# One drain for K instead of a masked double one, with the odd heads' rows copied by DMA

## The chip, the cores and the metric

The kernel runs on one core of a Trainium2 chip. The core has a matrix engine (TensorE, PE in the profile), which writes to PSUM, and three engines that compute on rows: VectorE (DVE), ScalarE (ACT) and GpSimd (POOL). SyncE (SP) issues the DMAs here. Each engine runs its own list of instructions in order and waits on semaphores for the others. The metric is the time of one execution on the device in microseconds; lower is better.

## What is computed

Two layers, applied twice in turn with the same weights, on x of 2048 tokens by 512, in bf16:

```python
def _A_ref(x, wqkv, wo):                       # attention; H = 32, Dh = 16, W = 256
    qkv = transpose((x @ wqkv).reshape(B, S, 3, H, Dh), 2, 0, 3, 1, 4)
    q, k, v = qkv[0], qkv[1], qkv[2]
    scores = jnp.einsum("bhqd,bhkd->bhqk", q, k) * (Dh ** -0.5)
    mask = (i - j >= 0) & (i - j < W)
    p = _softmax(jnp.where(mask, scores, -1e9))
    return (p @ v, heads joined) @ wo

def _B_ref(x, w1, b1, w2, b2):                 # MLP; F = 1792
    return _gelu(x @ w1 + b1) @ w2 + b2

x = x + _A_ref(_layernorm(x), A_wqkv, A_wo)
x = x + _B_ref(_layernorm(x), B_w1, B_b1, B_w2, B_b2)
x = x + _A_ref(_layernorm(x), A_wqkv, A_wo)
x = x + _B_ref(_layernorm(x), B_w1, B_b1, B_w2, B_b2)
```

Each query sees the 256 keys up to its own. There are 32 heads of only 16 dimensions.

## The kernel before

**Tiles.** x stays on chip (`X`). The two passes make 32 token tiles of 128 (tau = 0..31; 16 to 31 are the second pass), two tiles make an attention block (b = 0..15, blocks 8 to 15 the second pass). Per block: `lnq` normalises both tiles, transposes them into `xnTA` and projects Q into `QT`; `kv` projects K into `KT` and V into `Va`; `attention` does the scores, the exponential, the mask and the product with V; `outproj` adds the result to `X` and normalises for the MLP. The MLP runs in ten jobs (`JOBS`, J = 0..9) of two or four tiles (`mlp`).

**K and the heads.** `QT` and `KT` hold the head dimensions on the 128 partitions, four chunks c of 128, so a chunk has eight heads of 16 rows. The array is cut into pieces of 32 rows by 64 columns for the scores, and 32 rows hold two heads: rows 32r to 32r+15 the even one, 32r+16 to 32r+31 the odd one. For a score to see one head alone, the other head's rows of K must be zero. So `kv` writes K twice (line 1031): one VectorE instruction reads the PSUM bank [128, 512] twice, multiplies by `parmask` and writes `KT[:, kb, 0]` with the odd heads' rows zero and `KT[:, kb, 1]` with the even heads' rows zero. There are two such instructions per block (i = 0, 1, for chunks 2i and 2i+1), 32 in all. `KT` has two buffers (KB = 2): block b uses kb = b % 2.

**Scores.** A block's scores are one stream of positions, head pair by head pair, even (par 0) and then odd (par 1), cut into visits of 512 columns (`visit`; ten per block, six in blocks 7 and 15). A visit is 16 or 24 matmuls (8 per piece: two halves h, four row groups r) into four PSUM banks; two ScalarE exponentials of [128, 1024] take them to `E` (line 1112). Masks on `E` run on VectorE or GpSimd (line 1133). The product with V (`pv`) takes two phases per chunk pair and is transposed by VectorE (line 1198), normalised (1203, VectorE or GpSimd) and transposed again (1208).

**Layernorm.** `layernorm` computes mean and variance on VectorE (lines 934 and 936), variance + epsilon on VectorE (938), the power -0.5 on GpSimd (941), and the scaled row on VectorE (944). Layernorms ahead of the MLP of tiles 4 to 29 then go through DRAM: a transpose on VectorE into `xs_` (953), four DMAs into `scr_x` (957) and one from there into `xnTB` (961). All of those are on SP's queue.

**What sets the order.** The kernel builds 3295 operations with `add` (engine, function, an assumed duration, what is read and written, and possible other engines, `alt`). A written list, `ORDER` (line 635), gives the order in which they are put on their engines; x stands for operation x, and -1-x for operation x on its other engine. `_Plan.follow` goes through the list and picks PSUM banks; `_Sched` adds the semaphore waits that the reads and writes need. SP's DMAs use twelve semaphores in turn, and a DMA waits for the one twelve before it. `evac` (line 915) is the helper that drains a PSUM bank on VectorE (line 917) or, for the kinds in `ACT_OK`, on ScalarE (line 919).

Line 32 (`_Slots.matmul`) issues all matmuls, so the profile tells them apart by their tiles: `ps<-QT,KT` are scores, `ps<-E,Va` the product with V, `ps<-xnTA,Wqkv_sb` Q and K projections, `ps<-Wqkv_sb,xnTA` V, `ps<-Wo_sb,OT` the output projection, `ps<-xnTB,W_sb` and `ps<-W_sb,gT` the MLP.

Of the kernel before, what the change touches and what calls it, by code (L numbers as in the profile page):

```python
# [7 lines left out]
ALU = mybir.AluOpType  # L8
# [510 lines left out]
def bass_interleave_layers__sliding_block__dense_activation_gelu__prompt_kernel(  # L519
# [16 lines left out]
    Dh = 16  # L536
    H = D // Dh
    HC = P // Dh
    RG = HC // 2
# [7 lines left out]
    EPS = 1e-5  # L547
# [11 lines left out]
    KB = 2  # L559
# [20 lines left out]
    ACT_OK = "oqv"  # L580
# [12 lines left out]
    with ExitStack() as kctx:  # L593
        S_ = _Sched(nc, kctx)

        def sb(name, shape, dtype=dt.bfloat16):
# [275 lines left out]
        def dma(fn, writes, reads=(), dur=2200.0, prio=0.0, issue=640.0):  # L872
            add("sp", fn, dur, reads=reads, writes=writes, prio=prio, dma=True, geo=issue)
# [486 lines left out]
```

## Time and profile before

| | us |
|---|---|
| time, median of 3 runs | 459.97 (459.38 to 460.35) |
| the profiled execution's own time | 460.33 |
| its span, first to last instruction | 458.5 |
| PE busy | 442.5 |
| ACT busy | 394.7 |
| DVE busy | 362.1 |
| POOL busy | 257.6 |
| exponentials, 304 | 286.4, mean 1046 ns |
| K drains (line 1031), 32 | 38.6, mean 1211 ns |
| score matmuls, 2976 | 64.8 |
| DMA into scr_x, 104 of 32 KB, issue to landing | 1.6 |
| DMA into xnTB, 26 of 128 KB, issue to landing | 2.1 |

Busy times are those of the profiled execution; instructions that overlap are counted once, so 304 exponentials of 1046 ns fill 286.4 us. Matmuls overlap too: their distance from start to start is what they cost TensorE. A line of a group reads: line, engine, operation, output<-inputs, shape, count, then busy us and mean ns of one, then the engine's idle time just before them and what ended it. PEld is the load of a matmul's stationary side, which runs beside other matmuls.

### The profile page before, as it was taken

The page shows a single profiled execution, that of the slowest core. Times are in us where ns is not written, and L with a number is a line of the kernel's source. Part 1 is how long each engine was busy: PE and PEld are TensorE (multiplying, and loading weights), DVE is VectorE, ACT ScalarE, POOL GpSimd, SP SyncE. Part 2 cuts the span into 40 slices and gives each one's busy share as a digit, 9 for nine tenths or more (in the row PEclk, how much of TensorE's full clock was granted, in tenths as well). Part 3 has the DMA queues.
Part 4 walks back from the last instruction along what each step waited for, and adds up shares of the span by engine and source line. Part 5 has one row for each costly group of instructions (what it writes and reads, how often), then busy time and mean ns, then how long its engine had stood idle before and what let it go on. Part 6 is the DMA issues. An engine that isn't in the chain of part 4 may idle for free.

```text
span 458.5 us, 19397 instructions
## 1 busy us (share of the span) xinstructions
PE 442.5 (97%) x8793; PEld 235.6 (51%) x8793; DVE 362.1 (79%) x712; ACT 394.7 (86%) x475; POOL 257.6 (56%) x290
## 2 busy tenths in 40 slices
PE   7998899999889999999999999999999999999997
PEld 4554554655444455555445545556454554444663
DVE  5999888788997789886989788787787967777412
ACT  2999999999989989899997999979997999784442
POOL 4476665863656766664589464783556625563200
PEclk9999999999999999999999999999999999999999
DMA  7570000011010021100110102001020012002101
GB/s 229 195 279 4 4 3 3 5 18 33 16 34 3 9 44 23 29 11 17 26 49 3 24 14 48 16 9 44 11 51 3 11 40 40 23 5 70 59 23 59
DMA packets 27856, 18.18 MB, mean 40 GB/s; under 512 B 15868, under 2 KB 27260, under 8 KB 27772
## 3 DMA queue, kind: packets, MB, share of 16 engines
q1 hardware_dynamic: 27772, 16.92, 13.8%
q8 instruction: 69, 1.13, 1.0%
q14 instruction: 15, 0.12, 0.1%
HBM read 11.41 MB, written 5.51 MB: 37 GB/s over the span
## 4 chain that ended last, share of the span: by engine, by line
PE 71%; ACT 11%; DVE 9%; DMA 6%; SPq 2%; issue 1%; DVEq 0%
PE ps L32 70%; ACT E L1112 10%; DMA scr_x<-xs_ 2%; DMA xnTB<-scr_x 2%; DMA X<-in_A_x_dram 2%; DVE E L1133 1%; DVE stat L934 1%; PE ps L36 1%; SPq L957 1%; DVE KT L1031 1%; DVE Va L917 1%; DVE xn L944 1%; DVE xs_ L953 1%; ACT gT L1279 1%; DVE X L991 1%
## 5 line engine op out<-in xcount | busy, mean ns | idle before, releaser
L1112 ACT ACTIVATE E<-ps 128x1024 bf16<-128x1024 f32 x304 | 286.4, 1046 | 25.5 <-PE ps L32 24.6
L1133 POOL TENSOR_TENSOR E<-E,mask 128x512 bf16<-128x512 bf16 (+1 forms) x159 | 165.5, 1058 | 96.7 <-ACT E L1112 42.8
L32 PE MATMUL ps<-W_sb,gT 128*128 128x512 bf16 x448 | 117.6, 380 | 0.1
L32 PE MATMUL ps<-xnTB,W_sb 128*128 128x512 bf16 (+1 forms) x560 | 116.1, 337 | 1.2 <-DMA xnTB<-scr_x 0.8
L32 PEld LDWEIGHTS ps<-xnTB,W_sb 128*128 128x128 bf16 x560 | 50.7, 98 | 47.4 <-ACT E L1112 3.6
L991 DVE TENSOR_TENSOR X<-X,ps 128x512 bf16<-128x512 bf16 x64 | 43.4, 681 | 37.8 <-PE ps L32 37.2
L32 PE MATMUL ps<-QT,KT 32*64 32x320 bf16 (+4 forms) x2976 | 64.8, 258 | 6.0 <-ACT E L1112 5.3
L32 PE MATMUL ps<-xnTA,Wqkv_sb 128*128 128x256 bf16 x512 | 69.3, 274 | 1.0 <-DMA Wqkv_sb<-in_A_wqkv_dram 0.5
L1279 ACT ACTIVATE gT<-ps,b1T 128x512 bf16<-128x512 f32 (+1 forms) x92 | 48.7, 590 | 16.9 <-PE ps L32 16.4
L32 PEld LDWEIGHTS ps<-W_sb,gT 128*128 128x128 bf16 x448 | 39.5, 98 | 43.6 <-issue 5.9
L941 POOL TENSOR_TENSOR rstd<-veps,mhalf 128x1 f32<-128x1 f32 x64 | 36.8, 579 | 33.5 <-DVE veps L938 33.1
L32 PEld LDWEIGHTS ps<-xnTA,Wqkv_sb 128*128 128x128 bf16 x512 | 45.8, 98 | 18.9 <-issue 4.5
L32 PEld LDWEIGHTS ps<-QT,KT 32*64 32x64 bf16 x2976 | 27.2, 103 | 52.5 <-ACT E L1112 36.8
L1198 DVE STREAM_TRANSPOSE TT<-ps 128x1024 f32<-128x1024 f32 x32 | 39.9, 1246 | 14.2 <-PE ps L32 13.7
L32 PE MATMUL ps<-E,Va 64*17 64x128 bf16 (+3 forms) x3872 | 49.0, 230 | 1.8 <-POOL E L1133 0.5
L32 PEld LDWEIGHTS ps<-E,Va 64*17 64x17 bf16 x3872 | 39.3, 85 | 18.9 <-PE ps L32 6.8
L1242 POOL TENSOR_TENSOR X<-X,b2b 128x512 bf16<-128x512 bf16 x32 | 37.4, 1173 | 17.5 <-DVE xn L944 7.5
L1133 DVE TENSOR_TENSOR E<-E,mask 128x512 bf16<-128x512 bf16 (+1 forms) x103 | 41.7, 432 | 6.7 <-ACT E L1112 6.3
L934 DVE BATCH_NORM_STATS2 stat<-X 128x6 f32<-128x512 bf16 x64 | 43.7, 686 | 3.8 <-DMA X<-in_A_x_dram 2.8
L1031 DVE TENSOR_TENSOR KT<-ps,parmask 128x1024 bf16<-128x1024 f32 x32 | 38.6, 1211 | 4.7 <-PE ps L32 4.5
L1267 DVE TENSOR_SCALAR gT<-ps,b1T 128x512 bf16<-128x512 f32 (+1 forms) x48 | 31.9, 673 | 6.6 <-PE ps L32 6.0
L32 PE MATMUL ps<-Wqkv_sb,xnTA 128*128 128x512 bf16 x128 | 35.3, 381 | 0.2 <-DVE Va L917 0.2
(49 smaller groups left out, 331.3 us busy)
## 6 DMA issues: line engine op xcount, KB each, us to landing
W_sb<-in_B_w_dram SPq DMA_DIRECT2D x2, 1792.0 KB, 12.8
scr_x<-xs_ SPq DMA_DIRECT2D x104, 32.0 KB, 1.6
xnTB<-scr_x SPq DMA_DIRECT2D x26, 128.0 KB, 2.1
out_dram<-X SPq DMA_DIRECT2D x16, 128.0 KB, 1.8
Wqkv_sb<-in_A_wqkv_dram SPq DMA_DIRECT2D x3, 512.0 KB, 6.7
X<-in_A_x_dram SPq DMA_DIRECT2D x3, 512.0 KB, 4.9
X<-in_A_x_dram SPq DMA_DIRECT2D x2, 256.0 KB, 2.9
Wo_sb<-in_A_wo_dram SPq DMA_DIRECT2D x1, 512.0 KB, 6.5
```

Source lines behind the costliest of these rows:

```text
L32: return self.e.matmul(*a, **k)
L36: return self.e.transpose(*a, **k)
L934: add("dve", lambda e, B: e.bn_stats(stat6[:, k6, :], X[:, t, :]), 590, reads=["X%d" % t], writes=["st%d" % k6], prio=prio)
L941: add("pool", lambda e, B: e.tensor_tensor(out=rstd[:, k : k + 1], in0=veps[:, k : k + 1], in1=mhalf[:], op=ALU.pow), 535, reads=["ve%d" % ...
L991: add("dve", lambda e, B: e.tensor_tensor(out=X[:, t, :], in0=X[:, t, :], in1=ps[:, B[g][0], :], op=ALU.add), d_psum(512), reads=["X%d" % ...
L1031: add("dve", lambda e, B, g=g, i=i: e.tensor_tensor(out=KT[:, kb, :, 2 * i : 2 * i + 2, :].rearrange("p a c q -> p a (c q)"), in0=ps[:, B[ ...
L1112: add("act", lambda e, B, g_=g_, gi=gi: e.activation(E[:, 2 * gi : 2 * gi + 2, e0 : e0 + 512], ps[:, B[g_][0] : B[g_][0] + 2, :], AF.Exp, ...
L1133: op = lambda e, B, Ew=Ew, Mw=Mw: e.tensor_tensor(out=Ew, in0=Ew, in1=Mw, op=ALU.mult)
L1198: add("dve", lambda e, B: e.transpose(TT[:, s].rearrange("p a c q d -> p (a c q d)"), ps[:, B[g][0] : B[g][0] + 2, :].rearrange("p a n -> ...
L1242: add("pool", lambda e, B: e.tensor_tensor(out=X[:, t, :], in0=X[:, t, :], in1=b2b[:], op=ALU.add), 1110, reads=["X%d" % t, "b2b"], writes ...
L1267: add("dve", lambda e, B, g=g, fc=fc: e.tensor_scalar(out=gT[:, fc, 0:M], in0=ps[:, B[g][0], 0:M], scalar1=b1T[:, fc : fc + 1], scalar2=No ...
L1279: add("act", lambda e, B, g=g, fc=fc: e.activation(gT[:, fc, 0:M], ps[:, B[g][0], 0:M], AF.Gelu_apprx_tanh, bias=b1T[:, fc : fc + 1], scal ...
```

## The change

From block 2 on (`KDMA`), K's PSUM bank is drained once, unmasked, into `KT[:, kb, 0]`, by `evac` on VectorE or ScalarE ("k" joins `ACT_OK`). The even heads' scores read rows 32r to 32r+15 of it only, 16 rows instead of 32. For the odd heads, four DMAs (one per row group r) copy rows 32r+16 to 32r+31 from `KT[:, kb, 0]` to `KT[:, kb, 1]`, where the other rows are still zero from blocks 0 and 1, which keep the masked form. Blocks 2 and 3 (`KBOTH`) copy after each half i, 16 rows x 2 chunks; later blocks copy all four chunks after the second half. That makes 64 DMAs more. A score of an odd head waits for the copies of its chunk, all four of them.

In `layernorm`, variance + epsilon may also run on GpSimd. The list `ORDER` is new, of 3359 entries. In it, 8 of the 28 single K drains are on ScalarE and 34 of the 64 variance + epsilon on GpSimd; of masks, 7 double and 3 single ones pass from GpSimd to VectorE, 5 normalisations (line 1203) from VectorE to GpSimd, and 2 V drains and 4 drains of transposed x from ScalarE to VectorE.

```diff
-    ACT_OK = "oqv"
+    ACT_OK = "oqvk"
+    KDMA = KB
+    KBOTH = 4
...
         ORDER = [
...
         ]
...
-            add("dve", lambda e, B: e.tensor_scalar(
-                out=veps[:, k : k + 1], in0=statmv[:, k, 1:2], scalar1=EPS, scalar2=None, op0=ALU.add), 75,
-                reads=["mv%d" % k], writes=["ve%d" % k], prio=prio - 300)
+            eps = lambda e, B: e.tensor_scalar(
+                out=veps[:, k : k + 1], in0=statmv[:, k, 1:2], scalar1=EPS, scalar2=None, op0=ALU.add)
+            add("dve", eps, 75, reads=["mv%d" % k], writes=["ve%d" % k], prio=prio - 300, alt=(("pool", eps, 130, 0.0),))
...
+                if b >= KDMA:
+                    evac(lambda B, i=i: KT[:, kb, 0, 2 * i : 2 * i + 2, :].rearrange("p c q -> p (c q)"),
+                         lambda B, g=g: ps[:, B[g][0], :], 512, ["ps:" + g], ["K%d_0_%d" % (kb, 2 * i + c) for c in range(2)],
+                         prio, free=[g], kind="k")
+                    lo = 2 * i if b < KBOTH else 0
+                    if i or b < KBOTH:
+                        for r in range(RG):
+                            dma(lambda e, B, lo=lo, hi=2 * i + 2, r=r: e.dma_start(
+                                KT[32 * r + Dh : 32 * r + 2 * Dh, kb, 1, lo:hi, :], KT[32 * r + Dh : 32 * r + 2 * Dh, kb, 0, lo:hi, :]),
+                                ["K%d_1_%d%s" % (kb, c, "abcd"[r]) for c in range(lo, 2 * i + 2)],
+                                reads=["K%d_0_%d" % (kb, c) for c in range(lo, 2 * i + 2)],
+                                prio=prio, dur=2200.0, issue=400.0)
+                    continue
...
-                        rd += ["K%d_%d_%d" % (kb, par, c)] + ["Q%d_%d" % (qi, c) for qi in qb]
+                        rd += (["K%d_1_%d%s" % (kb, c, x) for x in "abcd"] if par else ["K%d_0_%d" % (kb, c)]) + ["Q%d_%d" % (qi, c) for qi in qb]
...
-                                rows = slice(32 * r, 32 * r + 32)
+                                rows = slice(32 * r, 32 * r + (32 if par or b < KDMA else Dh))
```

More of the change, by code (lines that the diff above doesn't have):

```diff
@@ L1029, in kv @@
                 prio = kprio + pair[i]
-                proj(g, 1, i, xs, xr, prio, ["K%d_%d_%d" % (kb, par, 2 * i + c) for par in range(2) for c in range(2)], "m1" if b < 1 else "o")
+                proj(g, 1, i, xs, xr, prio, ["K%d_0_%d" % (kb, 2 * i + c) for c in range(2)] + ["K%d_1_%d%s" % (kb, 2 * i + c, x) for c in range(2) for x in "abcd"], "m1" if b < 1 else "o")
+                if b >= KDMA:
[11 more added lines that the diff above has]
+                    continue
                 add("dve", lambda e, B, g=g, i=i: e.tensor_tensor(
@@ L1035, in kv @@
                     reads=["ps:" + g, "parmask"],
-                    writes=["K%d_%d_%d" % (kb, par, 2 * i + c) for par in range(2) for c in range(2)],
+                    writes=["K%d_0_%d" % (kb, 2 * i + c) for c in range(2)] + ["K%d_1_%d%s" % (kb, 2 * i + c, x) for c in range(2) for x in "abcd"],
                     prio=prio, free=[g])
```

362 rows, old and new, of the table ORDER are left out of this document.

## The prediction

> **What bounds the kernel now.** I read the page first, then busy time by stage, then the waits, then the timeline at the places where the waits lie. Page, parts 1 and 4 (busy shares; the chain that ended last):
>
> ```profile
> span 458.5 us, 19397 instructions
> PE 442.5 (97%) x8793; PEld 235.6 (51%) x8793; DVE 362.1 (79%) x712; ACT 394.7 (86%) x475; POOL 257.6 (56%) x290
> ...
> PE 71%; ACT 11%; DVE 9%; DMA 6%; SPq 2%; issue 1%; DVEq 0%
> ```
>
> VectorE, the engine that the change unloads, carries 9% of the chain. Where the chain lies is seen in the busy time of three stretches (us, then busy us of PE, PEld, DVE, ACT, POOL):
>
> ```profile
> 0.00:13.50 13.50, 10.95 (x82) 6.27 (x83) 8.39 (x24) 4.62 (x7) 5.06 (x20) 1.00 0.63 199
> 13.50:131.00 117.50, 108.11 (x2537) 62.41 (x2542) 106.28 (x227) 114.91 (x140) 74.38 (x80) 1.00 0.19 57
> 131.00:459.00 328.00, 323.48 (x6184) 166.97 (x6184) 247.41 (x463) 275.13 (x330) 178.11 (x191) 1.00 0.11 27
> ```
>
> From the first exponential (13.5) to 131, ScalarE works 114.9 of 117.5 us: its queue sets the pace, and TensorE idles 9.4 us. From 131 on, TensorE works 323.5 of 328 us, and 2.9 us of the rest lie behind the last matmul (residual, output). The clock is 1.00 everywhere. What TensorE waited for from 131 on (total, times, longest):
>
> ```profile
> PE ps L32 <- DMA xnTB<-scr_x: 0.8, 2, 0.5
> PE ps L32 <- ACT E L1112: 0.6, 1, 0.6
> PE ps L32 <- DVE Va L917: 0.2, 1, 0.2
> ```
>
> So only 1.6 us can be won there by shorter waits; K's drain is not among them. ScalarE's own waits between 13.5 and 131:
>
> ```profile
> ACT E L1112 <- PE ps L32: 1.9, 4, 1.0
> ACT QT L919 <- PE ps L32: 0.5, 2, 0.3
> ```
>
> **The change part by part.** The order list names every operation by its number in build order, a negative entry choosing the other engine; counting both lists gives what moves.
>
> *K's drain.* Rows (mean ns after the bar's busy us):
>
> ```profile
> L1031 DVE TENSOR_TENSOR KT<-ps,parmask 128x1024 bf16<-128x1024 f32 x32 | 38.6, 1211 | 4.7 <-PE ps L32 4.5
> L917 DVE CAST Va<-ps 128x512 bf16<-128x512 f32 x22 | 14.8, 676 | 1.0 <-PE ps L32 0.8
> L919 ACT ACTIVATE Va<-ps 128x512 bf16<-128x512 f32 x10 | 6.1, 612 | 0.0
> L938 DVE TENSOR_SCALAR veps<-statmv 128x1 f32<-128x1 f32 x64 | 9.0, 146 | 1.1
> ```
>
> Blocks 0 and 1 keep the masked form (4 drains). The other 28 x 1.211 = 33.9 us become 20 x 0.676 = 13.5 on VectorE, by V's row (same shapes), and 8 x 0.612 = 4.9 on ScalarE. VectorE: -20.4.
>
> *Other moves between engines.* The variance + epsilon of 34 of 64 layernorms goes to GpSimd: -34 x 0.146 = -5.0 on VectorE. On GpSimd its price lies between a memset of one column (0.10) and the power that follows it (0.58); nearest is its tensor_scalar on 128x64, 0.24, so +8 us on an engine idle 44%. Per layernorm that is 0.1 us later (-0.05 to +0.43), the hop between engines being only moved. Ten masks (+4.0 on VectorE at 0.43 and 0.30, -10.1 on GpSimd), five normalisations (-3.9 and +5.3), and two V drains and four transposed-x drains from ScalarE (+3.0; -3.7 there) change too. VectorE ends near 340 us, ScalarE near 396. VectorE's 22 us lie beside TensorE from 131 on and beside ScalarE before that, so I cost them at nothing directly; where that cover is thin is term 3.
>
> *Term 1, TensorE's own work.* Matmul counts and columns are the same. What differs is how often the array changes between full, score and P·V shape, and what that costs (start us, us, tile, count):
>
> ```profile
> 116.73 1.03 PE L32 MATMUL ps<-Wo_sb,OT 128*128 128x512 bf16 x4
> 117.69 0.43 PE L32 MATMUL ps<-QT,KT 32*64 32x64 bf16 x24
> ...
> 123.88 1.71 PE L32 MATMUL ps<-E,Va 64*17 64x256 bf16 x128 [0.17 <-ACT E L1112]
> 125.71 0.42 PE L32 MATMUL ps<-QT,KT 32*64 32x256 bf16 x16
> ...
> 135.53 0.80 PE L32 MATMUL ps<-E,Va 64*17 64x256 bf16 x64
> 136.26 0.42 PE L32 MATMUL ps<-QT,KT 32*64 32x256 bf16 x16
> ...
> 452.37 3.19 PE L32 MATMUL ps<-W_sb,gT 128*128 128x512 bf16 x14
> ```
>
> In the last line, 13 starts take 3.19 - 0.38, so 0.216 each; the four above take 0.96 to the next group, 0.094 more than 4 x 0.216. The old order has 374 changes, the new one 361; 7 of the 13 go before block 6, where ScalarE sets the pace, and 6 after: -0.56. One more pair of P·V phases stands back to back there: two together (x128) took 1.83 to the next group, two alone (x64) 2 x 0.73, so up to +0.37. Sum -0.2 (-0.6 to +0.2).
>
> The score matmuls of even heads contract 16 rows instead of 32. No row has a 16-row score. The nearest is the bias transpose, 14 rows: its weight load took 91 ns beside 98 with 128 rows. I take 0; the other end is a rival.
>
> *Term 2, ScalarE's stretch.* One V drain (0.61) leaves its queue early and one K drain (block 6) enters it before 131: 0. Of the 2.4 us that it waits for scores, the longest wait (1.0) follows 3.2 us of TensorE work between two score groups near 107; the new order puts 2.5 there. It also puts one more K projection step (0.22) ahead of the very first scores. I take -0.8 (-2.4 to +1.0). It reaches the end, because TensorE waits for ScalarE until 131.
>
> *Term 3, drains less late after 131.* Bounds: 0 and the 1.6 us of waits. K's drain frees its bank 0.53 us sooner and VectorE has less queued; the two waits for xnTB hang on a DMA chain that stays. I take -0.5.
>
> *Term 4, the 64 copies (added).* Four per block (eight for blocks 2 and 3), each 16 partitions x 2 KB (1 KB in blocks 2 and 3), on SP's queue and nowhere else. SP's price and the landing, from the timeline of SP and the page:
>
> ```profile
> 383.07 3.15 SPq L957 DMA_DIRECT2D scr_x<-xs_  x7
> ...
> scr_x<-xs_ SPq DMA_DIRECT2D x104, 32.0 KB, 1.6
> ```
>
> 0.45 us per issue and 1.6 to landing for the same 32 KB; the longest such landing in the chain is 3.4. SP issues in order, so behind a copy that waits for K's drain stand the layernorm's writes to scr_x and the reads into xnTB, and behind those stands the MLP; the odd heads' scores wait for four landings. Rows for cover: the new order leaves 4.6 us of TensorE work between block 9's last K matmul and its first odd-head score, 6.2 for block 12, 7 to 8 for blocks 10 and 11, over 10 for most others. Block 9's chain is 0.05 + 0.68 + 4 x 0.45 + 1.6 = 4.1: covered by 0.5. In front of MLP job 7's inputs stand up to four copies (1.8 us), but its writes wait for VectorE as well. I take +0.3 (0 to +4.7, worked out below).
>
> [...]
>
> **Sum:** -0.2 - 0.8 - 0.5 + 0.3 = -1.2 us on the profiled execution, whose time is 460.33 (span 458.5 and 1.8 around it), so 459.1. The median shown is 459.97, 0.36 lower; against it the forecast is **458.8**. About 0.2%, 0.92 us, is what a measurement of this kernel can tell from no change.
>
> **Rivals.**
> *Copies late (slower).* Place: block 9's first odd-head scores and the inputs of MLP jobs. If landings take 3.4 us and the drain queues 0.7, block 9's chain is 6.6 against 4.6 (+2.0), block 12's 6.6 against 6.2 (+0.4), job 7 loses up to 1.8, and the last of block 15's copies, issued behind job 7's writes, up to 0.5: +4.7 at worst. Half to two thirds, 3.3, with terms 1 and 2: 459.97 - 1.0 + 3.3 = 462.3. It decides from landings of about 2.1 us. For it: xnTB landings of 2.0 to 4.0 in the chain; against it: 1.6 as the median of this size.
> *Hidden anyway (same).* ScalarE's queue keeps its length, so terms 2 and 3 vanish: 459.97 - 0.2, with copies near +0: 459.7. For it: both stretches are full on an engine that the change does not unload.
> *VectorE was the cause early (faster by more).* Between 20 and 60 us VectorE is busy 38.0 of 40; three K drains (1.6) and some twelve epsilons (1.8) leave that stretch: about -3, so 456.9. Against it: ScalarE is as busy there, 39.5 of 40.
> *Sixteen rows count as another shape (slower).* A score group then changes shape where it passes from even to odd heads: 6 times per block, 60 times from block 6 on, 60 x 0.094 = +5.6; the 24 earlier lie under ScalarE: 465.3. Against it: the 14-row load.
> [...]
>
> **How the numbers follow.** Forecast 0.36 (its own range 457.5 to 459.05), VectorE early 0.08, hidden anyway 0.24, copies late 0.25, sixteen rows 0.07. The range leaves out sixteen rows, the far part of late copies (about 0.08) and of the early gain (0.03): **456.3 to 463.3**. Faster by over 0.2% (under 459.05): 0.36 + 0.08 = 0.44; within 0.2%: 0.24; slower: 0.25 + 0.07 = 0.32.
>
> **What would show it.** Term 1: 32x64 and 16x64 score matmuls with the same mean, and 0.094 at 361 changes; a longer score group means sixteen rows. Term 2: ScalarE's waits for scores before 131 under 2 us. Term 3: TensorE idle from 131 on not above 4.5 us. Term 4: no line of TensorE waiting for a DMA into KT, and the waits for xnTB near 0.8. VectorE near 340 us busy would show that the edit did what it says even if the time stands still. Wrong it would be if the order leaves TensorE short of ready work at places that the counts don't show: the new list moves most entries by a little, and I worked out only the thinnest covers.

## The result and the profile after

The changed kernel takes 465.74 us (median of 4 runs, 465.33 to 468.97) against 459.68 for the kernel before (median of 4, 458.75 to 460.35). It is slower by some 6 us, where the forecast was 1.2 us faster and the range ended at 463.3. The ratio is 1.0149, 95% interval 1.010 to 1.0198. Ratios here and below are those of the means, so this one stands for 6.8 us; differences in us are those of the medians, unless said otherwise.

The profiled execution is the slowest of the four, 468.97 us. Its page, parts 1 and 4 (busy time by engine; the chain that ended last):

```profile
span 467.2 us, 19397 instructions
PE 438.8 (94%) x8728; PEld 239.6 (51%) x8793; DVE 342.3 (73%) x681; ACT 396.2 (85%) x477; POOL 259.5 (56%) x319
...
PE 61%; ACT 26%; DMA 6%; DVE 3%; SPq 2%; issue 2%; DVEq 0%
```

VectorE and ScalarE came out as worked out (340 and 396 were forecast). (65 matmul records are missing in this trace, so that PE's busy time is a little too small, and "issue" in the waits below is mostly these holes.) The edited operations, line by line, from the groups of the changed kernel:

```profile
L923 DVE CAST KT<-ps 128x512 bf16<-128x512 f32 x20 | 13.4, 678 | 9.8 <-PE ps L32 9.6
L925 ACT ACTIVATE KT<-ps 128x512 bf16<-128x512 f32 x8 | 5.0, 619 | 0.0
L944 POOL TENSOR_SCALAR veps<-statmv 128x1 f32<-128x1 f32 x34 | 7.8, 232 | 20.6 <-DVE statmv L942 20.5
KT<-KT SPq DMA_DIRECT2D x48, 32.0 KB, 2.0
```

The three prices on the engines are those of the prediction (676, 612 and 240 ns). A copy lands in 2.0 us where 1.6 was taken, and its issue takes SP 0.59 us (median) where 0.45 was taken. So the edit did what it says, and the loss has to be looked for in waits and in the clock. The two long stretches of before:

```profile
13.50:131.00 117.50, 106.76 (x2522) 63.48 (x2537) 101.28 (x219) 114.36 (x138) 73.29 (x92) 0.98 0.20 59
131.00:459.00 328.00, 316.64 (x6118) 167.86 (x6169) 231.67 (x441) 275.57 (x329) 180.08 (x205) 0.98 0.13 30
```

The third number from the end is the clock granted to TensorE. It was 1.00 everywhere before; now it is 0.98 in both. What TensorE waited for from 131 us on (total, times, longest), and what ScalarE waited for between 13.5 and 131:

```profile
PE ps L32 <- DMA KT<-KT: 2.3, 2, 2.1
PE ps L32 <- DVE TT L1217: 1.4, 2, 1.2
PE ps L32 <- DMA xnTB<-scr_x: 0.8, 2, 0.6
...
ACT E L1131 <- PE ps L32: 2.6, 7, 0.8
```

The two upper lines are new: one late copy, and two waits put down to VectorE's transpose (`TT`, line 1217). For the longer of these two, 1.22 us at 415.8, it is not shown that the transpose is the cause; more on it further down. ScalarE waits for scores 2.6 us where it was 1.9. The worst place, in TensorE's timeline and in that of SP's queue:

```profile
394.04 0.80 PE L32 MATMUL ps<-E,Va 64*17 64x256 bf16 x64
396.96 0.65 PE L32 MATMUL ps<-QT,KT 16*64 16x256 bf16 x24 [2.11 <-DMA KT<-KT]
```

```profile
387.62 4.97 SPq L963 DMA_DIRECT2D scr_x<-xs_  x7
392.64 0.43 SPq L967 DMA_DIRECT2D xnTB<-scr_x  x1
393.11 0.51 SPq L1044 DMA_DIRECT2D KT<-KT  x1
```

The last copy of block 15 is issued at 393.11, behind seven writes of job 7's layernorm that take SP 5 us (3.0 us of issue, and one wait for VectorE). It lands 3.7 us later, where the median is 2.0 (in these microseconds the DMA engines are 48% busy, with the reads into `xnTB` around it), and TensorE stands still for 2.1 us. Most of that is the long landing: had the copy landed in 2.0 us, at 395.1, TensorE would have stood some 0.4 us (an estimate from these numbers; it had stopped at 394.84, and went on 0.14 us behind the landing). The clock around this place and around the stall at 127 us (window, PE, PEld, DVE, ACT, POOL, clock, DMA share, GB/s):

```profile
127.22:130.63 3.41, 1.84 (x42) 0.99 (x40) 3.41 (x9) 3.06 (x4) 1.36 (x2) 1.00 0.30 49
130.63:134.05 3.42, 2.82 (x49) 1.35 (x34) 0.97 (x2) 3.10 (x4) 2.25 (x3) 0.50 0.41 96
...
393.46:396.87 3.41, 1.32 (x66) 0.76 (x65) 1.94 (x3) 1.18 (x2) 1.29 (x2) 1.00 0.48 130
396.87:400.28 3.41, 2.99 (x37) 1.25 (x46) 0.39 (x1) 1.94 (x2) 0.91 (x1) 0.50 0.00 0
```

Here two windows of 3.41 us in which TensorE works little (1.84 and 1.32 us of it) are each followed by one at half clock (0.50). There are four windows at 0.50 in this execution (from 52.1, two from 130.6, one from 396.9); before, there is none inside the span. Such waits were paid twice, then: once as idle time and once, in some executions, as slower matmuls behind them (24 scores take 0.65 us at 396.96 and 0.43 at 401.97), up to 1.7 us for each window (an estimate: half of 3.41). The prediction's sum had no such term.

### The profile page after: what moved, and what is told of

Same layout as the page of the kernel before. It is cut to its first block, busy times and chain, and to the rows that moved or that the text cites. A ratio compares the mean times of both kernels' runs of the same rounds, so it can differ in the third digit from the quotient of the medians.

```text
span 467.2 us, 19397 instructions
## 1 busy us (share of the span) xinstructions
PE 438.8 (94%) x8728; PEld 239.6 (51%) x8793; DVE 342.3 (73%) x681; ACT 396.2 (85%) x477; POOL 259.5 (56%) x319
## 4 chain that ended last, share of the span: by engine, by line
PE 61%; ACT 26%; DMA 6%; DVE 3%; SPq 2%; issue 2%; DVEq 0%
PE ps L32 60%; ACT E L1131 20%; ACT gT L1298 3%; DMA scr_x<-xs_ 2%; ACT gT L1289 2%; DMA Wqkv_sb<-in_A_wqkv_dram 1%; SPq L963 1%; DMA KT<-KT 1%; DMA xnTB<-scr_x 1%; ACT L1289 1%; PE ps L36 1%; DVE X L997 1%; ACT L1131 1%; DVE TT L1217 1%; DVE E L1152 0%
## 5 line engine op out<-in xcount | busy, mean ns | idle before, releaser
L1152 POOL TENSOR_TENSOR E<-E,mask 128x512 bf16<-128x512 bf16 (+1 forms) x149 | 155.7, 1063 | 111.4 <-ACT E L1131 41.4
L32 PE MATMUL ps<-xnTB,W_sb 128*128 128x512 bf16 (+1 forms) x560 | 118.0, 343 | 1.5 <-DMA xnTB<-scr_x 0.8
L32 PE MATMUL ps<-W_sb,gT 128*128 128x512 bf16 x414 | 108.0, 383 | 3.8 <-issue 3.1
L32 PEld LDWEIGHTS ps<-xnTB,W_sb 128*128 128x128 bf16 x560 | 52.1, 99 | 46.6 <-issue 4.1
L32 PE MATMUL ps<-QT,KT 32*64 32x320 bf16 (+9 forms) x2976 | 66.6, 262 | 7.7 <-ACT E L1131 2.8
L32 PE MATMUL ps<-xnTA,Wqkv_sb 128*128 128x256 bf16 x512 | 70.7, 276 | 2.0 <-DMA Wqkv_sb<-in_A_wqkv_dram 1.1
L32 PEld LDWEIGHTS ps<-QT,KT 32*64 32x64 bf16 (+1 forms) x2976 | 28.3, 104 | 53.6 <-ACT E L1131 34.3
L1152 DVE TENSOR_TENSOR E<-E,mask 128x512 bf16<-128x512 bf16 (+1 forms) x113 | 47.0, 449 | 11.2 <-ACT E L1131 11.1
L1222 POOL TENSOR_TENSOR TM<-TT,Rc 128x512 bf16<-128x512 f32 x22 | 23.3, 1058 | 21.9 <-DVE Rc L1220 17.0
L32 PE MATMUL ps<-Wo_sb,OT 128*128 128x512 bf16 x115 | 31.5, 379 | 2.6 <-issue 1.3
```

Of the source, the lines that this page charges most:

```text
L32: return self.e.matmul(*a, **k)
L1152: op = lambda e, B, Ew=Ew, Mw=Mw: e.tensor_tensor(out=Ew, in0=Ew, in1=Mw, op=ALU.mult)
L1222: mul = lambda e, B: e.tensor_tensor(out=TM[:, sm].rearrange("p c q a d -> p a (c q) d"), in0=TT[:, s, :, :, :, 0:Dh].rearrange("p a c q d ...
```

## The experiments

Two theories stood at the start. "Waits": the new order and the copies make TensorE wait at new places, and the clock falls behind the longest. "Rows": the scores over 16 rows make TensorE slower. Then the question was which of copies, order and queue makes the waits. All ratios are against the kernel before on the same chip.

**Sixteen rows alone.** The kernel before, with its masked drains and its order; K's even rows are read without the zero rows.

```diff
-    rows = slice(32 * r, 32 * r + 32)
+    rows = slice(32 * r, 32 * r + (32 if par or b < KB else Dh))
```

> The kernel before with one edit: from block 2 on the even heads' scores contract 16 rows instead of 32 (K is still masked, so the result is the same). Theory 'rows' (16-row scores count for less in whatever halves the granted clock, and that is where the time went): clock of 0.985 to 0.995, some windows of 3.4 us at 0.5, time 462 to 466. Theory 'waits' (the new order runs into new waits, and the clock falls after the longest of them): clock 1.00 and the time of before, 459 to 460.5.

Measured: 460.22 (median of 10), ratio 1.0004 (0.9987 to 1.002). Sixteen rows cost nothing and bring nothing; "rows" falls, and with it the rival that sixteen rows count as another shape. In this run's groups by form:

```profile
L32 PE MATMUL ps<-QT,KT 32*64 32x320 bf16 x512 | 20.6, 297 | 0.1
L32 PE MATMUL ps<-QT,KT 16*64 16x320 bf16 x384 | 15.9, 308 | 1.6 <-ACT E L1112 1.5
```

**Thirty-two rows in the changed kernel.** The reverse.

```diff
-    rows = slice(32 * r, 32 * r + (32 if par or b < KDMA else Dh))
+    rows = slice(32 * r, 32 * r + 32)
```

> The changed kernel with one edit: the even heads' scores contract all 32 rows again, so they add the odd head's product (the scores of even heads are not the reference's; order, copies and drains stay). Theory 'rows': the clock is back at 1.00 and about 5 us are won, 459 to 462. Theory 'waits': as the changed kernel, 464.5 to 467, clock 0.985 to 0.993, with the wait of 2.1 us for the copy of block 15.

Measured: 464.24, ratio 1.0093 (1.0057 to 1.0128). Two of its four runs had the full clock and took 462.7 and 462.8; the other two, at a mean clock of 0.993 and 0.996, took 465.7 and 465.8. So 2.7 us of the loss are there at full clock (462.75, the middle of the two, against 460.06), and the executions in which the clock fell took about 3 us more. The median lies between the two expectations; what "rows" asked for, the full clock in general, isn't there.

The stall of 2.1 us at block 15, which "waits" expected here, is not there either. SP's queue and TensorE at that place:

```profile
392.55 0.51 SPq L1044 DMA_DIRECT2D KT<-KT  x1
```

```profile
394.72 0.43 PE L32 MATMUL ps<-QT,KT 32*64 32x256 bf16 x24
```

The copy stands behind the same seven writes (387.57 to 392.03), but lands in 1.98 us (at 394.53), and the scores go on without a wait. The stall of 2.1 us belongs to the execution that was profiled of the changed kernel, then, and not to the place alone.

**Block 15's copies first.** In the changed kernel's list, block 15's four copies are put right behind its K drains.

> The changed kernel with one move on SP's queue: the four K copies of block 15 stand right behind its K drains instead of among the layernorm's writes for MLP job 7. Theory 'waits': the wait of 2.1 us before block 15's scores is gone and with it the halved clock that follows (up to 1.7 us), so 462 to 463.8; up to 0.9 us comes back as job 7's inputs are later. Theory 'rows': 2.1 us at most are won, 463.6 to 464.5, and the clock still falls near that place.

Measured: 465.07, ratio 1.011 (1.009 to 1.013); 463.96 in the profiled execution, with the clock at 0.999. Both expectations are missed (464.5 at most). No scores of block 15 wait, but the time hardly moves: waits for `xnTB` stand at jobs 2 and 5 (1.2 and 0.9 us), and the clock falls in three of the four executions. One late copy is not the cause by itself.

This profile and that of the thirty-two rows show what a fall of the clock costs. TensorE's waits between 110 and 160 us, with thirty-two rows:

```profile
PE ps L32 <- DVE TT L1217: 1.4, 2, 1.2
PE ps L32 <- DMA xnTB<-scr_x: 1.2, 1, 1.2
```

With block 15's copies first, these two waits are the same in all their numbers (the transpose stands at line 1221 there). In the first profile the clock is at 0.50 for two windows, from 129.9 on, in the second it stays at 1.00. From the end of the 100th exponential to that of the 120th the first takes 34.1 us, the second 32.1, the kernel before 31.2. So these waits cost 0.9 us, and the two windows 2.0 us more.

**The order of before, with all edits.** The list of before; each copy right behind its K drain.

> The changed kernel's edits in the order of before: single drains (all on VectorE), copies right behind each block's last drain, 16-row scores, variance + epsilon on VectorE as before. Theory 'waits' (it is the new order): 458.5 to 461, clock 1.00. Theory 'rows' or any cost of the edits themselves: 462 or more, with a clock under 1.00.

Measured: 491.6, ratio 1.0695 (1.0677 to 1.0712). Theory "waits" in this form, by which the new order is to blame (458.5 to 461), is refuted: without the new order the change would cost five times as much. TensorE waits for the MLP's inputs:

```profile
PE ps L32 <- DMA xnTB<-scr_x: 15.7, 3, 6.7
```

**Without the copies, new and old order.** The copies are left out, the rest stands; once in the order of the changed kernel, once in the order of before.

```diff
-    lo = 2 * i if b < KBOTH else 0
-    if i or b < KBOTH:
-        for r in range(RG):
-            dma(...)
     continue
```

> The changed kernel in its new order, with the 64 copies of K's odd rows left out and nothing else changed. It leaves out the odd heads' K from block 2 on: their scores read the rows that blocks 0 and 1 left, and the output is another one; the work of TensorE, VectorE and ScalarE is the same. Theory 'copies' (the time is lost behind copies, by scores that wait for a landing and by the layernorm's writes behind them on SP's queue): 460 or less, and the waits of TensorE for a bank drained by VectorE go as well, since they would follow from the late start. Theory 'order' (the new order runs into new waits for banks and MLP inputs by itself): the copies' own stalls go (about 2 us, block 15 above all), the others stay, 462 to 463 with the clock at 1.0, and windows of half clock still follow the longest waits.

> All edits, in the order of before, with the copies left out. It leaves out the odd heads' K from block 2 on in the same way. K's single drain stands where the masked one stood. Theory 'copies': 459 to 460, VectorE some 14 us less busy, since K's drain was not among TensorE's waits. Theory 'order': the same number, so this run is the ground for the next one: what it lies above 460 is not the copies'. If it comes out below 459, a shorter drain is worth something by itself, which the prediction put at 0 to -0.8.

Measured: 460.98 in the new order, ratio 1.0027 (1.0007 to 1.0046), and 463.24 in the old one, 1.0079 (1.006 to 1.0099). The first number lies between its two expectations and splits the loss: without its copies the changed kernel is 1.0 us slower than before (1.2 by the ratio, whose interval is 0.3 to 2.1), so of the 6.1 us the copies make about 5. Part of the 1.0 is the clock's: the four of ten executions at clock 1.00 took 458.94 to 460.92, those in which it fell 460.57 to 462.98. The new order's own waits remain there, as theory "order" had it, but they are small:

```profile
PE ps L32 <- ACT E L1123: 3.1, 9, 0.6
PE ps L32 <- DVE TT L1209: 1.4, 2, 1.2
```

The comparison is clean: all runs in the new order have the same lists of the compute engines and the same PSUM banks for all 675 groups of matmuls, and the layernorm's DMAs stand in the same order on SP's queue. Against the kernel before, the changed kernel has other banks for 533 of the 675 groups beside its new order; no run separates these two.

The second number was a surprise to both theories: work taken away from VectorE, nothing added, and 3.2 us more. Comparing what the planner decided for the two lists shows a side effect: it assumes a shorter drain, so it believes banks to be free earlier, and picks other PSUM banks than before for 234 of the 675 groups. The run with all copies in the old order (491.6) had the same fault.

**Only SP's queue in the new order.** VectorE, ScalarE, GpSimd and TensorE in the order of before.

> All edits with the copies. VectorE, ScalarE, GpSimd and TensorE work in the order of before; only SP's queue stands in the order of the changed kernel. All copies right behind their drains, in the order of before, gave 491.6. Theory 'queue' (what costs is the place of the copies on SP's queue, in front of the layernorm's writes): most of the 31 us goes, 461 to 466. Theory 'landing' (the copies cost because odd heads' scores come too soon behind K in the order of before, wherever the copies stand on SP): 475 or more, with TensorE waiting for copies into KT.

Measured: 497.37, ratio 1.0811 (1.0776 to 1.0847), the slowest of all. The "queue" theory in this form is refuted: this order of SP's queue isn't good by itself. It has to fit the order in which the other engines produce what it moves; here TensorE waited 9.0 us for `xnTB` and, as "landing" had it, 8.8 us for copies. (Its banks differ from those of before too, so it says nothing finer.)

**The banks put back.** As the run without copies in the order of before, but the planner goes on assuming the masked drain's duration, so that all 675 groups get the banks of before; and the same order and banks with the copies.

```diff
-    evac(..., 512, ["ps:" + g], ["K%d_0_%d" ...], prio, free=[g], kind="k")
+    add("dve", lambda e, B, g=g, i=i: e.tensor_copy(KT[:, kb, 0, ...], ps[:, B[g][0], :]), d_psum(1024) + 10, ...)
```

```diff
                 t, got = best
+                got = self.banks[len(self.took)]
+                self.took.append(got)
...
```

> As the run without copies in the order of before (463.2), with one thing put back: the planner assumes the duration of the old masked drain for the new one, so that it picks the PSUM banks of before (in that run 234 of 675 groups had got other banks, because the planner believed in earlier drains). It leaves out the odd heads' K from block 2 on. Theory 'banks' (the 3.2 us of that run came from the banks): 459 to 460.3. Theory 'drain' (a single drain at the place of the masked one is itself no good, whatever the banks): 462.5 to 463.5 again.

> All edits with the 64 copies right behind their drains, in the order of before and with the banks of before, which are given as a list. Theory 'queue' (the copies hold up the layernorm's writes and reads behind them on SP's queue, and K's landings hold up odd heads' scores): 485 to 492, as with the other banks (491.6), with TensorE waiting for xnTB and KT. Theory 'banks': a large part of those 31 us was the banks' doing, under 475.

Measured: 459.63 without copies, ratio 0.9992 (0.9971 to 1.0012): theory "banks" holds, and the drain's 12 us of VectorE time (350.2 busy against 362.1) are worth nothing here. With copies 485.64, ratio 1.0575 (1.0544 to 1.0607), as "queue" had it: so 26 us are the copies' and, by difference, 5.5 of the 31.5 the banks'. The chain can be read at 359 us. SP's queue, TensorE, and the granted clock in the run with copies:

```profile
359.25 2.65 SPq L1070 DMA_DIRECT2D KT<-KT  x4
361.95 1.52 SPq L989 DMA_DIRECT2D scr_x<-xs_  x3
```

```profile
366.68 1.89 PE L32 MATMUL ps<-xnTB,W_sb 128*128 128x512 bf16 x4 [6.65 <-DMA xnTB<-scr_x]
```

```profile
362.90:366.30 3.40, 0.00 (x0) 0.00 (x0) 0.00 (x0) 0.00 (x0) 1.19 (x2) 0.50 0.30 68
366.30:369.70 3.40, 3.02 (x74) 1.41 (x74) 0.75 (x1) 0.00 (x0) 0.00 (x0) 0.50 0.00 0
```

SP finished a write at 353.3 and then stood until 359.25, when the second of the two drains of K ended, although the three writes behind the copies had had their data since 352 (both tiles' transposes had ended by then). The MLP's read, issued at 364.66, waits for those writes, TensorE waits 6.65 us for the read, and then works at half clock.

**Copies that nobody reads.** The changed kernel with every copy in its place on SP's queue; the odd heads' scores read the unmasked rows.

```diff
-    rd += ([... "K%d_1_%d%s" ...] if par else ["K%d_0_%d" % (kb, c)]) + ...
+    rd += ([... "K%d_1_%d%s" ...] if par and b < KDMA else ["K%d_0_%d" % (kb, c)]) + ...
-    KT[rows, kb, par, c, ...]
+    KT[rows, kb, par if b < KDMA else 0, c, ...]
```

> The changed kernel with all its copies at their places on SP's queue, but from block 2 on no score reads what they write: the odd heads' scores read the unmasked rows that the drain wrote, 32 of them, so it leaves out the separation of the two heads of a pair. SP's queue is as long as before this edit, and only the scores' wait for landings is gone. Theory 'queue' (the 4.8 us between the changed kernel and the one without copies, 461.0, are spent by DMAs behind copies): 464 to 466, with TensorE's waits for xnTB and half-clock windows still there. Theory 'landing' (the scores' own waits for copies, block 15's above all): 461 to 462.

**Copies up to block 6 only.** In the changed kernel, `if i or b < KBOTH` becomes `if (i or b < KBOTH) and b < 7`.

> The changed kernel with the copies of blocks 2 to 6 alone; those of blocks 7 to 15 are left out, and with them the odd heads' K of these blocks (their scores read what earlier blocks left). Copies before about 140 us remain, copies after it are gone. Theory 'early' (most of the 4.8 us is lost by 140 us, at MLP job 2's inputs and by the clock behind it): 464 or more. Theory 'late' (most is lost by single late places afterwards: jobs 5 and 6, block 15): 461 to 462.5. In the profiled run of the changed kernel the excess over the one without copies was 1.3 us between 40 and 60 us, 1.8 between 120 and 140, and 3.2 between 380 and 400.

Measured: 463.22 for both; ratios 1.0067 (1.0045 to 1.0088) and 1.0078 (1.0047 to 1.0109). Each lies between its two expectations. Copies that only occupy SP's queue cost 3.6 - 1.0 = 2.6 us, and that scores wait for them (and what the clock adds) costs the other 2.5. This split is rough: by the ratios it is 1.8 and 3.8 us, with intervals of about 1 us on each number. (The unmasked rows are read 32 at a time for odd heads, as in the changed kernel.) The copies up to block 6, where ScalarE still sets the pace, make about half of what the copies cost (3.6 - 1.0 us again). What unread copies do is seen at MLP job 2, SP's queue with the copies and without them:

```profile
103.09 14.24 SPq L1044 DMA_DIRECT2D KT<-KT  x4
...
121.38 3.00 SPq L967 DMA_DIRECT2D xnTB<-scr_x  x2
124.47 4.37 SPq L963 DMA_DIRECT2D scr_x<-xs_  x8
```

```profile
106.56 0.85 SPq L967 DMA_DIRECT2D xnTB<-scr_x  x2
...
122.79 4.53 SPq L963 DMA_DIRECT2D scr_x<-xs_  x8
```

The group of four copies that begins at 103.09 is spread over 14.24 us: two of block 4's are issued, then SP stands until block 5's K drain ends at 116. Behind it in the list stand writes of the layernorm that the run without copies had issued by 105.5. So the first two reads come at 121 and 124 instead of 107, the eight writes of the next two tiles 1.7 us later, and the last reads 1.5 us later (129.56 and 128.04). TensorE waits 1.18 us for them at 132.4. (In the profiled execution without copies the clock had fallen at 128, so the wait itself can't be compared there; the next run was profiled at full clock, as this one.)

**SP's queue sorted anew.** All edits, all copies read, every compute engine in the changed kernel's order. Only SP's list changes: the layernorm's DMAs by the moment at which the run without copies issued them, the copies by the end of K's drain. The layernorm's DMAs keep their order among themselves by this; only the 64 copies change their places.

> All edits with the 64 copies; every compute engine works in the changed kernel's order and only SP's queue is sorted anew: each DMA stands where its data is ready in the run without copies (the layernorm's by the moment that it was issued there, the copies by the end of K's drain). Block 5's copies so move behind the writes and reads that were ready before K's drain, and block 15's last one in front of job 7's writes. Theory 'queue' (copies cost by where they stand among the layernorm's DMAs): the stalls at block 15 (2.2 us) and at job 2's inputs (0.5 to 0.8 more than without copies) go, 461 to 463; it can't come under the run without copies, 461.0. Theory 'load' (64 more DMAs cost by their number and landings, wherever they stand): 464 to 466.

Measured: 461.91 (median of 12), ratio 1.0056 (1.0035 to 1.0078). "Queue" holds, "load" falls: the same 64 copies, put where their data is ready, cost 1 us instead of 5, and as the interval of the run without copies (1.0007 to 1.0046) overlaps this one, even the 1 us isn't certain. The interval of the changed kernel (1.010 to 1.0198) lies clear of both. SP's queue at the place that was late before, and TensorE's waits in the whole run:

```profile
116.47 2.42 SPq L1048 DMA_DIRECT2D KT<-KT  x4
123.03 5.17 SPq L967 DMA_DIRECT2D scr_x<-xs_  x8
128.93 0.85 SPq L971 DMA_DIRECT2D xnTB<-scr_x  x2
```

```profile
PE ps L32 <- DVE TT L1221: 2.6, 3, 1.2
...
PE ps L32 <- DMA xnTB<-scr_x: 0.5, 2, 0.3
...
PE ps L32 <- DMA KT<-KT: 0.2, 1, 0.2
```

TensorE waits for a copy once, for 0.2 us, and the longest wait for `xnTB` is 0.3 us, where it was 1.18 with the copies unread. The waits put down to `TT` are the new order's own. Nothing here beats the kernel before. In the order and with the banks of before the shorter drain wins nothing either: even with the copies for nothing it stands at 0.9992.

## Why the prediction was wrong, step by step

The step that failed by most is term 4: the copies were taken at +0.3 us (0 to 4.7), and they cost 5.1. Beside it the gains of terms 2 and 3, taken at -1.3 us, did not reach the end of the run. The sum, term by term (medians against the kernel before on the same chip):

| step of the prediction | forecast, us | measured |
|---|---|---|
| K's drain, veps, masks: VectorE 340, ScalarE 396, worth nothing by themselves | 0 | 342.3 and 396.2; K's drain alone, in the order and banks of before: ratio 0.9992; veps and masks not measured alone |
| term 1: shape changes and 16 rows | -0.2 | 16 rows: +0.2 (ratio 1.0004); the 13 changes not measured alone |
| terms 2 and 3: ScalarE's stretch, drains less late | -1.3 | with term 1: +1.0 (new order, no copies) |
| term 4: the copies | +0.3 (0 to 4.7) | 5.1 (5.6 by the ratios), of it some 4 by their places on SP's queue |
| the clock | no term | inside the two rows above |

**What bounds the kernel** was read rightly, and so were the costs of the single operations on the engines. That VectorE's time is worth nothing, which the prediction took from the chain and the waits, is shown directly for 12 of the 20 us, those of K's drain.

**Term 1** is in line with the runs as far as they go. For sixteen rows the prediction took 0, from the weight load of a 14-row tile (91 ns beside 98), and the trace of sixteen rows alone agrees: matmul means of 308 and 297 ns, and no change of the time (ratio 1.0004).

**Terms 2 and 3** failed. In the new order without copies ScalarE's waits for scores did shrink, by more than the 0.8 taken, from 1.9 and 0.5 to 1.3:

```profile
ACT E L1123 <- PE ps L32: 1.3, 3, 0.8
```

Part of the gain arrived and was lost again. The 100th of the 304 exponentials ends 0.6 us earlier than in the kernel before without copies, and 0.3 earlier with SP's queue sorted (128.15 in the kernel before). By the 120th, near 159 us, that is gone. In between stands a wait of 1.2 us for a PSUM bank that the transpose `TT` empties, in front of block 5's first scores; in the kernel before the same scores wait 0.64 us. The last exponential, near 408 us, ends 0.1 us later than in the kernel before in both runs, and the rest of the loss comes behind it (0.7 and 1.0 us at the end of the span), where TensorE stands still around an output projection. With SP's queue sorted, PEld, TensorE and VectorE at this place:

```profile
406.91 0.32 PEld L32 LDWEIGHTS ps<-Wo_sb,OT 128*128 128x128 bf16 x2
408.45 0.38 PE L32 MATMUL ps<-Wo_sb,OT 128*128 128x512 bf16 x1 [1.16 <-DVE TT L1221]
...
407.06 1.25 DVE L1221 STREAM_TRANSPOSE TT<-ps 128x1024 f32<-128x1024 f32 x1 [0.35 <-PE ps L32]
```

The profile puts the 1.16 us down to `TT`, but the load of the weights, which stands behind the projection's wait for VectorE (the kernel issues a wait ahead of the matmul that it is for), started at 406.91, before the transpose began at 407.06. What VectorE had to finish for it was the drain that frees the projection's bank, and that ended at 406.71. In the changed kernel it is the same projection:

```profile
415.84 0.38 PE L32 MATMUL ps<-Wo_sb,OT 128*128 128x512 bf16 x1 [1.22 <-DVE TT L1217]
```

So the cause of this stall is open. In seven profiles of the new order a 16 KB transfer on the queue that the page calls "instruction" begins 2.2 to 2.8 us before TensorE goes on here (in the changed kernel's at 413.4, 2.4 us before); whether the stall hangs on it no run tests. What failed in terms 2 and 3 is that they counted shorter waits at the old places and gave new places no time. The prediction's last sentence named this, an order that leaves TensorE short at places that counts don't show.

**Term 4** had the right mechanism, in the rival "copies late", and the wrong size. What the sum counted was the issue time of copies (0.45 us each) and their landing; what they cost is the time for which SP stands in front of one whose data isn't ready, with the layernorm's DMAs behind it. The same copies, sorted by readiness, cost 1 us. The rival was to decide from landings of about 2.1 us; the median is 2.0, the longest 7.8.

Of the rival's places the first, block 9's odd scores (up to 2.0), waited 0.2 us. The second, the inputs of MLP jobs, waited as it says: at job 2 0.6 to 1.2 us with all copies in place, at job 5 0.2 to 0.9. The third, "the last of block 15's copies, issued behind job 7's writes, up to 0.5", stalled for 2.1 us in one profile, by a landing of 3.7 us, and not at all in another with the same queue. The rival's 462.3 is near the runs at full clock with most of these waits (462.4 for copies unread, 462.7 and 462.8 with 32 rows). That is in part luck: it had most of its 3.3 us at block 9.

**What was in no term** is the clock. The changed kernel's four runs had a mean granted clock of 0.985 to 0.993; the 57 runs of the kernel before beside the experiments had 0.999 or 1.00, but for two at 0.996. In the run with SP's queue sorted, executions at full clock took 461.2 to 461.9, those at 0.996 461.1 to 462.6, and those at 0.988 to 0.993 463.9 to 466.3. The last are 2 to 5 us longer, and with it the time passes the end of the range, 463.3, which was made of waits alone. In the one place where the waits are the same with and without a fall, two windows at half clock cost 2.0 us.

"Hidden anyway", the rival in which the gains vanish and the copies are covered, describes the new order without copies but for 1.2 us (-0.2 forecast, +1.0 measured); "VectorE early" has nothing for it.

Open is how the copies' 5 us split between SP's queue, scores that wait and the clock behind both: the falls differ from execution to execution, and no run holds the clock fixed.

## What to carry to other kernels

Count a DMA that is added to an in-order queue by what stands behind it while its data isn't ready, not by its issue and its landing: the same 64 copies cost 26 us behind their drains in the old order, 5 in the new one, and 1 when sorted by readiness. When TensorE bounds the kernel and already runs at 97%, price new waits at more than their length: here the clock fell behind some of them, and two windows at half clock cost 2.0 us beside the 0.9 us of the waits themselves. And before a planner's durations are changed, see what else hangs on them: here a shorter assumed drain alone moved a third of the PSUM banks and cost 3.2 us.

## What was not expected of the hardware

In the changed kernel's profile, with TensorE busy 438.8 of 467.2 us, the granted clock fell to 0.50 three times inside the span: for 3.41 us from 52.12, for 6.83 from 130.63 and for 3.41 from 396.87, the last behind a stall of 2.11 us. The windows of 3.41 us in front of the last two had 1.84 and 1.32 us of work. A busy share alone does not settle it: behind the changed kernel's window from 48.71, with 2.20 us of work, it fell, and with block 15's copies first it did not fall behind the window from 130.02, with 1.82. The falls come at other moments in every profile (128.2, 129.9, 130.6 and 131.6 in four of the new order, behind the same stretch), and the same waits are followed by a fall in one profile and not in another (thirty-two rows, and block 15's copies first); the four runs of the changed kernel spread over 3.6 us, the four of the kernel before in the same comparison over 1.6.

The landing of one copy differs as well: 3.71 us in one execution and 1.98 in another, at the same place of the same queue, and the longest of the 32 KB and 16 KB copies in the changed kernel's profile took 7.8 us.
